# Folding the forward transform over d twice, rounding the spectrum on 128 rows at once, and a product over s1 on alternating halves of the partitions

## The chip, the cores and the metric

One core of one Trainium2 chip runs the whole program. The metric is the device time of one execution in microseconds. Beside it stands the span of one profiled execution, from its first to its last instruction. The engines are named as in the profile: PE is TensorE's matmul, PEld its weight load, DVE is VectorE, ACT is ScalarE, SP is SyncE, which issues most of the DMAs.

## The reference

x has 2048 rows (s) of 576 columns (d). With xn the layer norm of x over d,

```
g = xn @ w_gate ; u = xn @ w_up                  # 576 -> 4608
glu = (sigmoid(g) * u) @ w_down                  # 4608 -> 576
X = rfft2(xn, axes=(s, d)) * (w_r + 1j * w_i)    # 2048 x 289 frequencies
out = x + irfft2(X) + glu
```

All data is float32 and the answer has to be close to float32.

## The kernel before

**Arithmetic.** A float32 matrix is rounded by ACT to a short float that TensorE takes at full rate (the high part), and DVE subtracts it from the original (the low part). A product is three products: high by high, low by high, high by low. Where only 32 rows of the contraction are left (REM), the three are stacked on 96 partitions (KR) and done in one.

**The gated unit** is most of the work: `unit` (L679) runs the products of one block of 128 hidden columns over a half of the rows (L648, 512 columns each), and `down` (L741) and `seven` (L831) the products with w_down (L755 and L846, 288 columns each). They run on PE from the start of the span to its end.

**The spectral branch** runs beside it in the second half of the rows. `begin` (L874) gives the round in which each of its generators starts; in each round every active generator is taken one step further, to its next `yield`. So a `yield` is the distance of one group of 7 matmuls of the gated unit and what goes with it, and the order in which the instructions are written is the order of the rounds. The tile framework then orders each engine's instructions at build time by that order and by its own costs; an instruction whose operands aren't ready there is passed by later ones. On the chip each engine runs its list in order.

`phase1b(t)` (L462) is the forward part for row tile t, of 16: one tile holds two values of s2 with 64 values of s1 each.

- It loads 288 pairs of columns of x, transposed (xs), and the mean of each row spread over the partitions (mb, L467).
- Fold over d (L475 to L477): difference and sum of x[d] and x[575-d], the mean taken off the sums. Of 288 values each 256 lie on 128 partitions twice, 32 on the stacked rows.
- High and low part (fh, fl; L480 to L483).
- Product over d (pd, L486 to L493): for real (e = 0) and imaginary part (e = 1) seven matmuls of 290 columns: two blocks of 128 rows by three, and the 96 stacked rows. The columns are the frequencies, the odd ones first (144), then an empty column that makes 290 of 289, then the 145 even ones. The constants are `cf`.
- Rounding of the spectrum (L496 to L502): pd has s2 and s1 on the partitions and the parts in two PSUM banks. The next product wants part and s1 on the partitions, so four times 64 partitions are moved, each by one ACT (ah) and one DVE instruction (al), scaled by the layer norm's 1/std.
- Product over s1 (pa, L505 to L508): for each of the two s2 three matmuls over 128 partitions, with `am`.
- ACT copies pa to SBUF (L510), and it goes to DRAM (L511).

The tiles pd and pa come from `pair` (L171): two places of two PSUM banks each, shared with the products of L755 and L846.

`phase2` does the sum over s2, the filter and its inverse. `phase3` does the way back; its product over d (pe, L598 to L604) is already folded twice: for each part one matmul of 288 columns over the 102 stacked rows, and six of 144 columns over 128 rows.

At the very start, before x has come, PE multiplies the identity (L902 to L904), some of it with 64 rows: H0 are partitions 0 to 63 and H1 are 64 to 127, taken in turn and written to two different banks.

Of the kernel before, what the change touches and what calls it, by code (L numbers as in the profile page):

```python
# [68 lines left out]
def _constants():  # L69
    out = {}  # L70

    mid = np.arange(HD) - (D - 1) / 2
    ang = 2 * np.pi * mid[:, None] * KOF[None, :] / D
    t = np.zeros((P, 2, 5, NQ), np.float32)
    for e, v in ((0, np.cos(ang)), (1, -np.sin(ang))):
        m = np.where(FREQ, v, 0.0)
        hi, lo = _split(m)
        for part, w in ((0, hi), (1, lo)):
            t[:, e, 2 * part] = w[:P]
            t[:, e, 2 * part + 1] = w[P:2 * P]  # L80
        t[:KR, e, 4] = np.concatenate([hi[2 * P:], hi[2 * P:], lo[2 * P:]])
    out["cf"] = t.reshape(P, 10 * NQ)
# [52 lines left out]
def _layout(x, w_r, w_i, w_gate, w_up, w_down):  # L135
# [11 lines left out]
    lay = {"x": x.reshape(NT, P, D), "xt": xt.reshape(NT, P, 2 * (KT + 1) * P), "xg": xg, "ri": v.reshape(N2 // 2, P, 4 * NQ),  # L147
# [1089 lines left out]
```

## Time and profile before

| | us |
|---|---|
| median of 3 runs (lowest, highest) | 1418.54 (1418.04, 1419.33) |
| the profiled execution | 1417.6 |
| its span | 1415.8 |
| PE busy | 1400.5 (99%) |
| PEld busy | 1228.9 (87%) |
| DVE busy | 1123.7 (79%) |
| ACT busy | 640.3 (45%) |

A matmul's duration in the profile reaches from its issue to the end of its way through the array, and the next one starts before that end. So busy times of PE add up to more than the work, and a cost is read from start to start.

### The profile page before, as it was taken

What the parts mean: (1) busy time and instruction counts of PE and PEld (TensorE: products, weight loads), DVE (VectorE), ACT (ScalarE), POOL (GpSimd) and SP (SyncE); (2) the same over time, 40 slices, a digit from 0 to 9 for tenths busy, and PEclk for the clock granted to TensorE, in tenths of its full rate; (3) what the DMA queues carried; (4) which work ended last, traced back from release to release, by engine and by line L of the source; (5) the groups of instructions that cost most, each with busy time, mean ns of one, the idle gap of its engine ahead of it and who ended that gap; (6) DMA issues with size and microseconds to landing.
All of it is one profiled execution on the core that took longest, in us unless ns stands there. A gap on an engine that the chain in (4) does not pass through costs nothing. (4 is left out here: it accounts for less than half of the span.)

```text
span 1415.8 us, 20731 instructions
## 1 busy us (share of the span) xinstructions
PE 1400.5 (99%) x7883; PEld 1228.9 (87%) x7883; DVE 1123.7 (79%) x1736; ACT 640.3 (45%) x1035; POOL 3.3 (0%) x5
## 2 busy tenths in 40 slices
PE   7999999999999999999999999999999999999998
PEld 5888888888888888888888888888888889888887
DVE  7988888888888888789466888877878878777885
ACT  6644444444444444444245444434555534443431
POOL 0000000000000000000000000000000000000000
PEclk9999999999999999999999999999999999999999
DMA  7588677777777776665777777778888787776643
GB/s 251 194 330 306 257 271 261 271 261 270 262 270 261 272 262 243 246 250 176 274 213 237 225 234 222 219 244 266 274 269 271 241 278 223 242 221 205 194 127 84
DMA packets 131043, 342.54 MB, mean 242 GB/s; under 512 B 12192, under 2 KB 51648, under 8 KB 126208
## 3 DMA queue, kind: packets, MB, share of 16 engines
q1 hardware_dynamic: 130016, 339.91, 71.7%
q8 instruction: 62, 1.02, 0.3%
q10 hardware_dynamic: 928, 1.31, 0.3%
q14 instruction: 37, 0.30, 0.1%
HBM read 205.04 MB, written 136.13 MB: 241 GB/s over the span
## 5 line engine op out<-in xcount | busy, mean ns | idle before, releaser
L648 PE MATMUL pB<-X,w 128*128 128x512 f32 x1484 | 381.0, 394 | 0.9 <-ACT pB L699 0.5
L648 PEld LDWEIGHTS pB<-X,w 128*128 128x128 f32 x1484 | 267.4, 188 | 51.7 <-ACT v L712 1.3
L648 PE MATMUL pE<-X,w 128*128 128x512 f32 x1064 | 272.3, 392 | 0.1
L648 PE MATMUL pA<-X,w 128*128 128x512 f32 x1008 | 259.3, 392 | 1.8 <-DVE X L455 1.2
L648 PEld LDWEIGHTS pE<-X,w 128*128 128x128 f32 x1064 | 193.1, 188 | 35.1 <-DVE y L713 0.7
L648 PEld LDWEIGHTS pA<-X,w 128*128 128x128 f32 x1008 | 182.7, 188 | 35.2 <-DVE X L455 1.9
L755 PE MATMUL po<-wd,hh 128*128 128x288 f32 x1216 | 210.8, 295 | 0.0
L846 PEld LDWEIGHTS ps<-wf,hs 128*128 128x128 f32 x1260 | 188.6, 188 | 18.5 <-ACT qs L854 0.9
L846 PE MATMUL ps<-wf,hs 128*128 128x288 f32 x1260 | 202.0, 295 | 0.4 <-ACT qs L854 0.4
L755 PEld LDWEIGHTS po<-wd,hh 128*128 128x128 f32 x1216 | 184.2, 188 | 11.7 <-ACT hh L738 0.4
L759 DVE TENSOR_TENSOR acc<-acc,po 128x576 f32<-128x576 f32 x168 | 125.7, 749 | 65.4 <-PE po L755 64.9
L250 ACT ACTIVATE w<-raw 128x768 fp32r<-128x768 f32 (+1 forms) x106 | 100.9, 953 | 92.6 <-PE pE L648 36.5
L755 PE MATMUL po<-wd,hl 128*128 128x288 f32 x608 | 128.7, 293 | 0.0
L856 DVE TENSOR_TENSOR qs<-qs,ps 128x576 f32<-128x576 f32 x112 | 84.0, 750 | 25.4 <-PE ps L846 24.4
L755 PEld LDWEIGHTS po<-wd,hl 128*128 128x128 f32 x608 | 98.7, 189 | 0.0
L713 DVE TENSOR_TENSOR y<-v,pE 128x512 f32<-128x512 f32 x68 | 46.6, 686 | 50.3 <-ACT v L712 49.5
L733 DVE TENSOR_TENSOR y<-y,g 128x1024 f32<-128x1024 f32 x67 | 81.9, 1222 | 3.4 <-DVE y L732 0.5
L782 ACT ACTIVATE hs<-y 128x512 fp32r<-128x512 f32 x105 | 64.8, 629 | 43.4 <-DVE y L820 14.8
L252 DVE TENSOR_TENSOR w<-raw,w 128x512 fp32r<-128x512 f32 (+1 forms) x106 | 81.8, 772 | 3.2 <-ACT w L250 2.9
L856 DVE TENSOR_TENSOR acc<-acc,ps 128x576 f32<-128x576 f32 x90 | 67.4, 750 | 19.5 <-PE ps L846 18.6
L716 ACT ACTIVATE g<-pB 128x512 f32<-128x512 f32 x68 | 40.7, 598 | 91.3 <-PE pB L648 91.3
L712 ACT ACTIVATE v<-pB 128x512 f32<-128x512 f32 x68 | 40.6, 597 | 70.5 <-PE pB L648 70.2
(170 smaller groups left out, 1611.0 us busy)
## 6 DMA issues: line engine op xcount, KB each, us to landing
w<-wsp SPq DMA_DIRECT2D x246, 320.0 KB, 3.6
wsp<-w SPq DMA_DIRECT2D x34, 2240.0 KB, 7.8
raw<-in_w SPq DMA_DIRECT2D x34, 768.0 KB, 9.6
wdsp<-wd SPq DMA_DIRECT2D x36, 576.0 KB, 4.6
wf<-tsp SPq DMA_DIRECT2D x60, 288.0 KB, 3.5
wf<-wdsp SPq DMA_DIRECT2D x45, 288.0 KB, 3.9
std<-in_wd SPq DMA_DIRECT2D x36, 288.0 KB, 5.5
ri<-in_ri SPq DMA_DIRECT2D x16, 580.0 KB, 5.1
```

Of the source, the lines that this page charges most:

```text
L250: placed(nc.scalar.activation(o[:, :, :3, :], src, AF.Copy))
L252: placed(nc.vector.tensor_tensor(o[:, :, 3:, :], src[:, :, :KT, :], f32(o[:, :, :KT, :]), op=OP.subtract))
L648: nc.tensor.matmul(bank, w[:, sw, :], X[:, x, sx, :], start=start and j == 0, stop=stop and j == len(STEPS) - 1, skip_group_check=skip)
L712: nc.scalar.activation(v[:, 1], bank["B"], AF.Copy)
L713: nc.vector.tensor_tensor(y[:, 1], v[:, 1], bank["E"], op=OP.add)
L716: nc.scalar.activation(g[:, 1], bank["B"], AF.Sigmoid)
L733: nc.vector.tensor_tensor(y, y, g, op=OP.mult)
L755: nc.tensor.matmul(pd[:, b, :HD], h[i], w[k][b], start=g == 0 and n == 0, stop=g == G - 1 and n == 2)
L759: nc.vector.tensor_tensor(a, a, pd[:, :, :HD], op=OP.add)
L782: nc.scalar.activation(hs[:, 0], src, AF.Copy)
L846: nc.tensor.matmul(pd[:, i, :HD], h[:, a, m], w[:, b], start=q == 0, stop=q == 2)
L856: nc.vector.tensor_tensor(o, o, pd[:, :, :HD], op=OP.add)
```

## The change

The fold is done twice. xs now comes as the four quarters of a row of x (the two that belong together at each level of the fold lie beside each other), and mb is no longer loaded. Two DVE instructions make sums and differences of 512 elements a partition, two of 256 elements and one with the sign column `sg` fold these once more. For each part the odd frequencies need one combination and the even ones the other, so a matmul of 290 columns over 128 rows becomes one of 144 and one of 146 columns, with half the rows in all. The mean only changes frequency 0: DVE takes 576 times the mean from that one column of pd. The spectrum is then rounded by one ACT and one DVE instruction on all 128 partitions. The product over s1 contracts over 64 partitions for one part and one s2 at a time: twelve matmuls instead of six, and from one to the next the half of the partitions and the PSUM bank change.

```diff
     ang = 2 * np.pi * (QTR[:, None] + 0.5) * KOF[None, :] / D     # constants
-    t = np.zeros((P, 2, 5, NQ), np.float32)
+    t = np.zeros((P, 2, 3, NQ), np.float32)
...
+    out["sg"] = np.where(np.arange(P) % REM < REM // 2, 1.0, -1.0).astype(np.float32)[:, None]
...
+    am = am.reshape(2, N1, N2 // 2, 2, 2, P).transpose(3, 1, 2, 0, 4, 5)
...
-    xt = x[:, np.argsort(COLS)].reshape(NT, P, 2, HD)
-    xt = np.stack([xt[:, :, 0], xt[:, :, 1, ::-1]], 2)
-    xt = xt[..., ks].reshape(NT, P, 2, KT + 1, P).transpose(0, 4, 2, 3, 1)
+    qs = np.concatenate([np.arange(P), np.tile(np.arange(P, HQ), P // (HQ - P))])
+    xt = x.reshape(NT, P, 2, 2, HQ)[..., qs].reshape(NT, P, 2, 2, 2, P).transpose(0, 5, 3, 2, 4, 1)
...
     def phase1b(t):
-        pool, cf = R["pool"], R["cf"]
-        xs = pool.tile([P, 2, KT + 1, P], F32, tag="xs", name=f"xs{t}", bufs=2)
-        nc.sync.dma_start(xs.rearrange("p h k s -> p (h k s)"), xt[t])
-        mb = pool.tile([P, P], F32, tag="mb", name=f"mb{t}", bufs=2)
-        nc.sync.dma_start(mb, rowd[0, t].partition_broadcast(P))
+        pool, cf, sg = R["pool"], R["cf"], R["sg"]
+        xs = pool.tile([P, 3, 2, 2 * P], F32, tag="xs", name=f"xs{t}", bufs=2)
+        nc.sync.dma_start(xs[:, :2].rearrange("p h j s -> p (h j s)"), xt[t])
         am = pool.tile([P, 2, 2, P], F32R, tag="am", name=f"am{t}", bufs=2)
         load_r(am, con["am"][:, t * 4 * P:(t + 1) * 4 * P].rearrange("p (a h m) -> p a h m", a=2, h=2))
         yield
         yield
         yield
         yield
-        eo = pool.tile([P, 2, KT + 1, P], F32, tag="eo", name=f"eo{t}")
-        tc.keep_in_program_order(nc.vector.tensor_tensor(eo[:, 1], xs[:, 0], xs[:, 1], op=OP.subtract))
-        nc.vector.scalar_tensor_tensor(xs[:, 0], mb.unsqueeze(1).to_broadcast([P, KT + 1, P]), -2.0, xs[:, 0], op0=OP.mult, op1=OP.add)
-        nc.vector.tensor_tensor(eo[:, 0], xs[:, 0], xs[:, 1], op=OP.add)
-        fh = pool.tile([P, 2, KT + 1, P], F32R, tag="fh", name=f"fh{t}")
-        fl = pool.tile([P, 2, KT, P], F32R, tag="fl", name=f"fl{t}")
+        tc.keep_in_program_order(nc.vector.tensor_tensor(xs[:, 2], xs[:, 0], xs[:, 1], op=OP.add))
+        nc.vector.tensor_tensor(xs[:, 0], xs[:, 0], xs[:, 1], op=OP.subtract)
+        v = xs[:, 0::2]
+        eo = pool.tile([P, 2, 3, P], F32, tag="eo", name=f"eo{t}")
+        six = eo.rearrange("p e c s -> p (e c) s")
+        for o, op in ((six[:, 0::4], OP.add), (six[:, 1::2][:, :2], OP.subtract)):
+            nc.vector.tensor_tensor(o, v[:, :, 0, :P], v[:, :, 1, :P], op=op)
+        nc.vector.scalar_tensor_tensor(eo[:, :, 2], v[:, :, 1, P:], sg, v[:, :, 0, P:], op0=OP.mult, op1=OP.add)
+        fh = pool.tile([P, 2, 3, P], F32R, tag="fh", name=f"fh{t}")
+        fl = pool.tile([P, 2, 2, P], F32R, tag="fl", name=f"fl{t}")
         nc.scalar.activation(fh, eo, AF.Copy)
-        nc.vector.tensor_tensor(fl, eo[:, :, :KT], f32(fh[:, :, :KT]), op=OP.subtract)
+        nc.vector.tensor_tensor(fl, eo[:, :, :2], f32(fh[:, :, :2]), op=OP.subtract)
         r = slice(REM, 2 * REM)
-        nc.vector.tensor_tensor(fh[r, :, KT], eo[r, :, KT], f32(fh[r, :, KT]), op=OP.subtract)
+        nc.vector.tensor_tensor(fh[r, :, 2], eo[r, :, 2], f32(fh[r, :, 2]), op=OP.subtract)
         yield
         yield
         pd = pair(f"pd{t}")
         for e in range(2):
-            steps = []
-            for k in range(2):
-                steps += [(fh[:, e, k, :], cf[:, e, k, :]), (fl[:, e, k, :], cf[:, e, k, :]), (fh[:, e, k, :], cf[:, e, 2 + k, :])]
-            steps.append((fh[:KR, e, KT, :], cf[:KR, e, 4, :]))
-            for n, (l, r) in enumerate(steps):
-                nc.tensor.matmul(pd[:, e, :NQ], l, r, start=n == 0, stop=n == len(steps) - 1)
+            nc.tensor.matmul(pd[:, e, :NQ], fh[:KR, 1 - e, 2, :], cf[:KR, e, 2, :], start=True, stop=False, skip_group_check=True)
+            for c, o in ((0, slice(0, HQ)), (1, slice(HQ, NQ))):
+                for n, (v, i) in enumerate(((fh, 0), (fl, 0), (fh, 1))):
+                    nc.tensor.matmul(pd[:, e, o], v[:, 1 - e, c, :], cf[:, e, i, o], start=False, stop=n == 2, skip_group_check=True)
         ah = pool.tile([P, 2, NQ], F32R, tag="ah", name=f"ah{t}", bufs=1)
         al = pool.tile([P, 2, NQ], F32R, tag="al", name=f"al{t}", bufs=1)
-        for sl in range(2):
+        zero = pd[:, 0, PAD + 1:PAD + 2]
+        nc.vector.scalar_tensor_tensor(zero, mv[:, t, 0:1], float(-D), zero, op0=OP.mult, op1=OP.add)
+        v, r = pd[:, :, :NQ], rstd[:, t:t + 1]
+        nc.scalar.activation(ah, v, AF.Copy, scale=r)
+        nc.vector.scalar_tensor_tensor(al, v, r, f32(ah), op0=OP.mult, op1=OP.subtract)
+        yield
+        yield
+        pa = pair(f"pa{t}")
+        for n, (h, m) in enumerate(((0, ah), (0, al), (1, ah))):
             for ci in range(2):
-                o = slice(ci * N1, (ci + 1) * N1)
-                i = slice(sl * N1, (sl + 1) * N1)
-                v, r = pd[i, ci, :NQ], rstd[i, t:t + 1]
-                nc.scalar.activation(ah[o, sl, :], v, AF.Copy, scale=r)
-                nc.vector.scalar_tensor_tensor(al[o, sl, :], v, r, f32(ah[o, sl, :]), op0=OP.mult, op1=OP.subtract)
-        yield
-        yield
-        pa = pair(f"pa{t}")
-        for sl in range(2):
-            for n, (h, m) in enumerate(((0, ah), (0, al), (1, ah))):
-                nc.tensor.matmul(pa[:, sl, :NQ], am[:, sl, h, :], m[:, sl, :], start=n == 0, stop=n == 2)
+                for sl in range(2):
+                    o = slice(sl * N1, (sl + 1) * N1)
+                    nc.tensor.matmul(pa[:, sl, :NQ], am[o, ci, h, :], m[o, ci, :], start=n + ci == 0, stop=n + ci == 3)
...
     def stage1():
         pool = room("1")
-        R["cf"] = cf = pool.tile([P, 2, 5, NQ], F32R, name="cf")
-        load_r(cf, con["cf"].rearrange("p (e k n) -> p e k n", e=2, k=5))
+        R["cf"] = cf = pool.tile([P, 2, 3, NQ], F32R, name="cf")
+        load_r(cf, con["cf"].rearrange("p (e k n) -> p e k n", e=2, k=3))
+        R["sg"] = sg = pool.tile([P, 1], F32, name="sg")
+        nc.sync.dma_start(sg, con["sg"])
```

## Rows read from the trace of the kernel before

**Rows 1.** The head of the page: span, busy time, share and instructions of each engine
```profile
span 1415.8 us, 20731 instructions
PE 1400.5 (99%) x7883; PEld 1228.9 (87%) x7883; DVE 1123.7 (79%) x1736; ACT 640.3 (45%) x1035; POOL 3.3 (0%) x5
```
**Rows 2.** The page's chain that ended last, by line
```profile
PE ps L846 10%; PE pB L648 10%; PE pE L648 6%; PE pA L648 6%; PE po L755 2%; PE pd L493 2%; PE pe L604 1%; PE pc L548 1%; PE py L575 1%; PE pb L532 1%; PE pa L508 1%; DVE al L502 1%; DVE hs L783 0%; PE pz L588 0%; DVE y L820 0%; PE pe L600 0%
```
**Rows 3.** By stretch: length, busy PE, PEld, DVE, ACT, POOL, clock, DMA share, GB/s
```profile
500.00:700.00 200.00, 199.90 (x1096) 175.63 (x1096) 155.73 (x218) 79.76 (x110) 0.00 (x0) 1.00 0.69 246
...
722.00:937.00 215.00, 213.49 (x1202) 184.47 (x1201) 175.21 (x287) 108.33 (x189) 0.00 (x0) 1.00 0.74 223
```
**Rows 4.** Groups by line, 722 to 937 us: PEld; after the bar busy, mean ns, idle before
```profile
L846 PEld LDWEIGHTS ps<-wf,hs 128*128 128x128 f32 x402 | 59.7, 188 | 6.9 <-ACT qs L854 0.9 <-DVE acc L856 0.8 <-ACT hs L782 0.4
...
L508 PEld LDWEIGHTS pa<-ah,am 128*128 128x128 f32 x64 | 11.3, 188 | 5.7 <-DVE al L502 2.9 <-ACT qs L854 0.9 <-ACT ah L501 0.8
L508 PEld LDWEIGHTS pa<-al,am 128*128 128x128 f32 x32 | 6.0, 189 | 0.8 <-DVE al L502 0.8
```
**Rows 5.** Timeline of PE, product over d of tile 0; columns: start us, length us
```profile
726.96 0.30 PE L493 MATMUL pd<-cf,fh 128*128 128x290 f32 x1
...
728.86 0.39 PE L648 MATMUL pE<-X,w 128*128 128x512 f32 x1
```
**Rows 6.** Busy time of L493, then of L508 alone (PE, PEld), columns as above
```profile
722.00:937.00 215.00, 35.58 (x224) 31.97 (x224) 1.00 0.74 223
...
722.00:937.00 215.00, 17.42 (x96) 13.61 (x96) 1.00 0.74 223
```
**Rows 7.** Timeline of PE, product over s1 of tile 0 and what follows
```profile
735.80 0.29 PE L508 MATMUL pa<-ah,am 128*128 128x290 f32 x1
...
736.62 0.39 PE L648 MATMUL pA<-X,w 128*128 128x512 f32 x1
736.85 0.29 PE L846 MATMUL ps<-wf,hs 128*128 128x288 f32 x1
```
**Rows 8.** Timeline of PE, the way back's product over d of tile 0
```profile
1172.31 0.30 PE L600 MATMUL pe<-drt,z3r 102*128 102x288 f32 x1
...
1172.52 0.27 PE L604 MATMUL pe<-dit,z3l 128*128 128x144 f32 x1
...
1173.08 0.34 PE L600 MATMUL pe<-drt,z3r 102*128 102x288 f32 x1
...
1173.88 0.44 PE L648 MATMUL pB<-X,w 128*128 128x512 f32 x1
```
**Rows 9.** Timelines of PE and PEld at the start, 8 to 10.1 us
```profile
8.02 0.19 PEld L904 LDWEIGHTS b<-idr 64*128 64x128 f32 x2 [0.65 <-issue]
8.36 0.63 PE L904 MATMUL b<-idr 64*128 64x512 f32 x4
8.59 0.83 PE L904 MATMUL b<-idr 64*128 64x512 f32 x3
8.92 0.19 PEld L904 LDWEIGHTS b<-idr 128*128 128x128 f32 x1 [0.37 <-issue]
9.59 0.18 PEld L904 LDWEIGHTS b<-idr 64*128 64x128 f32 x1 [0.37 <-issue]
10.02 0.19 PEld L904 LDWEIGHTS b<-idr 128*128 128x128 f32 x1 [0.24 <-issue]
```
**Rows 10.** Groups by line, 722 to 937 us: DVE and ACT
```profile
L502 DVE SCALAR_TENSOR_TENSOR al<-pd,rstd,ah 64x290 fp32r<-64x290 f32 x64 | 33.2, 519 | 19.5 <-ACT ah L501 18.1
...
L481 DVE TENSOR_TENSOR fl<-eo,fh 128x512 fp32r<-128x512 f32 x16 | 11.0, 687 | 2.0 <-ACT fh L480 1.8
...
L475 DVE TENSOR_TENSOR eo<-xs 128x384 f32<-128x384 f32 x16 | 8.9, 554 | 0.2
...
L501 ACT ACTIVATE ah<-pd,rstd 64x290 fp32r<-64x290 f32 x64 | 31.8, 498 | 46.4 <-PE pd L493 28.9 <-DVE al L502 16.6
...
L510 ACT ACTIVATE x<-pa 128x580 f32<-128x580 f32 x16 | 10.5, 654 | 19.6 <-PE pa L508 13.1 <-issue 6.4
```

More of the change, by code (lines that the diff above doesn't have):

```diff
@@ L70, in _constants @@
     out = {}
-    mid = np.arange(HD) - (D - 1) / 2
-    ang = 2 * np.pi * mid[:, None] * KOF[None, :] / D
-    t = np.zeros((P, 2, 5, NQ), np.float32)
-    for e, v in ((0, np.cos(ang)), (1, -np.sin(ang))):
-        m = np.where(FREQ, v, 0.0)
-        hi, lo = _split(m)
[L78 to L82, printed above, removed]
+    ang = 2 * np.pi * (QTR[:, None] + 0.5) * KOF[None, :] / D
+    t = np.zeros((P, 2, 3, NQ), np.float32)
+    for e, m in ((0, np.cos(ang)), (1, np.sin(ang))):
+        m = np.where(FREQ & (KOF != (HD, 0)[e]), m, 0.0)
+        hi, lo = _split(m)
+        t[:, e, 0], t[:, e, 1] = hi[:P], lo[:P]
+        even, odd = ~ODD, ODD
+        both = []
+        for v in (hi, hi, lo):
+            both += [v[P:] * w.astype(np.float32) for w in ((even, odd) if e == 0 else (odd, even))]
+        t[:KR, e, 2] = np.concatenate(both)
+    out["cf"] = t.reshape(P, 6 * NQ)
+    out["sg"] = np.where(np.arange(P) % REM < REM // 2, 1.0, -1.0).astype(np.float32)[:, None]
     s1 = np.arange(N1)
@@ L142, in _layout @@
     x = x.reshape(S, D)[ROWS][:, COLS]
-    xt = x[:, np.argsort(COLS)].reshape(NT, P, 2, HD)
-    xt = np.stack([xt[:, :, 0], xt[:, :, 1, ::-1]], 2)
-    xt = xt[..., ks].reshape(NT, P, 2, KT + 1, P).transpose(0, 4, 2, 3, 1)
+    qs = np.concatenate([np.arange(P), np.tile(np.arange(P, HQ), P // (HQ - P))])
+    xt = x.reshape(NT, P, 2, 2, HQ)[..., qs].reshape(NT, P, 2, 2, 2, P).transpose(0, 5, 3, 2, 4, 1)
     xg = x.reshape(NT, P, 2, HD)[TPP:, ..., ks].reshape(2, TPC, P, 2, KT + 1, P).transpose(0, 3, 5, 4, 1, 2).reshape(2, 2, P, (KT + 1) * CW)
-    lay = {"x": x.reshape(NT, P, D), "xt": xt.reshape(NT, P, 2 * (KT + 1) * P), "xg": xg, "ri": v.reshape(N2 // 2, P, 4 * NQ),
+    lay = {"x": x.reshape(NT, P, D), "xt": xt.reshape(NT, P, 8 * P), "xg": xg, "ri": v.reshape(N2 // 2, P, 4 * NQ),
            "w": w.reshape(NF, P, 4 * (KT + 1) * P), "wd": w_down[:, COLS].reshape(NF, P, D)}
@@ L487, in phase1b @@
         for e in range(2):
-            steps = []
-            for k in range(2):
-                steps += [(fh[:, e, k, :], cf[:, e, k, :]), (fl[:, e, k, :], cf[:, e, k, :]), (fh[:, e, k, :], cf[:, e, 2 + k, :])]
-            steps.append((fh[:KR, e, KT, :], cf[:KR, e, 4, :]))
-            for n, (l, r) in enumerate(steps):
-                nc.tensor.matmul(pd[:, e, :NQ], l, r, start=n == 0, stop=n == len(steps) - 1)
+            nc.tensor.matmul(pd[:, e, :NQ], fh[:KR, 1 - e, 2, :], cf[:KR, e, 2, :], start=True, stop=False, skip_group_check=True)
+            for c, o in ((0, slice(0, HQ)), (1, slice(HQ, NQ))):
+                for n, (v, i) in enumerate(((fh, 0), (fl, 0), (fh, 1))):
+                    nc.tensor.matmul(pd[:, e, o], v[:, 1 - e, c, :], cf[:, e, i, o], start=False, stop=n == 2, skip_group_check=True)
         ah = pool.tile([P, 2, NQ], F32R, tag="ah", name=f"ah{t}", bufs=1)
         al = pool.tile([P, 2, NQ], F32R, tag="al", name=f"al{t}", bufs=1)
-        for sl in range(2):
-            for ci in range(2):
-                o = slice(ci * N1, (ci + 1) * N1)
-                i = slice(sl * N1, (sl + 1) * N1)
-                v, r = pd[i, ci, :NQ], rstd[i, t:t + 1]
-                nc.scalar.activation(ah[o, sl, :], v, AF.Copy, scale=r)
-                nc.vector.scalar_tensor_tensor(al[o, sl, :], v, r, f32(ah[o, sl, :]), op0=OP.mult, op1=OP.subtract)
+        zero = pd[:, 0, PAD + 1:PAD + 2]
[3 more added lines that the diff above has]
+        nc.vector.scalar_tensor_tensor(al, v, r, f32(ah), op0=OP.mult, op1=OP.subtract)
         yield
@@ L505, in phase1b @@
         pa = pair(f"pa{t}")
-        for sl in range(2):
-            for n, (h, m) in enumerate(((0, ah), (0, al), (1, ah))):
-                nc.tensor.matmul(pa[:, sl, :NQ], am[:, sl, h, :], m[:, sl, :], start=n == 0, stop=n == 2)
+        for n, (h, m) in enumerate(((0, ah), (0, al), (1, ah))):
+            for ci in range(2):
+                for sl in range(2):
+                    o = slice(sl * N1, (sl + 1) * N1)
+                    nc.tensor.matmul(pa[:, sl, :NQ], am[o, ci, h, :], m[o, ci, :], start=n + ci == 0, stop=n + ci == 3)
         x1 = pool.tile([P, 2, NQ], F32, tag="x1", name=f"x1{t}", bufs=1)
```

## The prediction, written before the changed kernel was built or run

> **What bounds the kernel now.** I read the head of the page first: PE is busy for 1400.5 of 1415.8 us, DVE for 79%, ACT for 45% [rows 1]. The chain of waits, followed back from the end, goes through PE's lines, with 1% for the busiest line of another engine [rows 2]. So time is won or lost where PE's instructions get closer or further apart. The table by stretch, of a stretch without the spectral branch and of the one in which phase1b runs, says whether another engine takes over there: PE 213.49 of 215 us, DVE 175 (81%), ACT 108 (50%), DMA share 0.74, the clock at 1.00, which is 2.4 GHz [rows 3]. PE still sets the pace; DVE is near enough to delay it. What PE loses to them is read from the idle time ahead of its weight loads: 6.5 us ahead of the loads of pa, 6.9 us ahead of those of L846 [rows 4]. The forms and start times of the single instructions give the costs below.
>
> **The product over d.** Fourteen matmuls before and after. Before, they start at 726.96 us and the next product at 728.86: 1.90 us, 0.136 each [rows 5]. In ten of the sixteen tiles the first one starts early and the other 13 follow, with another product between, which makes 26 runs. PE's busy time at L493 is 35.58 us; each run reaches 0.16 us over the start of its follower (0.30 of duration less 0.14), so it is (35.58 - 26 x 0.16) / 16 = 1.96 us a tile [rows 5, 6]. After, each part is one matmul of 290 columns over 96 rows, three of 144 and three of 146. This has a twin: the way back's product, one of 288 columns over 102 rows and six of 144, twice, takes 1.57 us [rows 8]. It isn't half: from 1172.52 to 1173.08 five matmuls of 144 columns start, 0.112 us each, against 0.136 for 290 columns, so the narrow ones pay for something other than columns, and 146 should cost as 144 does. The product behind the twin lasts 0.44 instead of 0.39 us: its load comes 0.05 late. So 1.57 + 0.05 = 1.62, and 1.96 - 1.62 = 0.34 a tile, 5.5 us over 16. Ends: 6.2 (1.57) and 2 (the first matmul now needs the last DVE result, the stacked rows' low part, so a load that waits could cost 0.2 a tile more; but until it is ready PE has other products, and the split falls away).
>
> **The product over s1.** Six matmuls become twelve over 64 rows. Before: 0.82 us where nothing waits (735.80 to 736.62) [rows 7]; (17.42 - 19 x 0.16) / 16 = 0.90 on average, in 19 runs [rows 6]. The trace has 64-row matmuls on alternating halves of the partitions and alternating banks at the start, 512 columns wide. Pairs of them start at 8.36 and 8.59 us: 0.23 a pair [rows 9], which is what one over 128 rows takes (736.62 to 736.85) [rows 7]. So the two of a pair run side by side, and twelve of 290 columns cost six passes, 0.82, as before.
>
> Each change of mode costs extra, though. Three pairs take from 8.02 to 8.92, 0.90 us, where 3 x 0.23 = 0.69: 0.21 over. Two matmuls over 128 rows from there to 9.59: 0.67 for 0.46, 0.21 over. One pair from there to 10.02: 0.43 for 0.23, 0.20 over [rows 9]. At every one of these points the load is preceded by an idle time put down to "issue", and isn't ahead of its matmul as elsewhere. One visit is two changes, 0.41 us; 16 visits are +6.6 us.
>
> The Trainium skill has a rule that speaks against this edit: in "TensorEngine Tiling (Array Packing)", under Tiling Modes, Key Properties, it says that changing the tiling mode, other than changing the tile, drains TensorE. The trace agrees, with 0.20 to 0.21 us a change [rows 9]; the page has no price. Without this rule and these rows the switch term would be nothing and the sum below 6.6 us lower, 1410.8.
>
> Two things go with it. First the waits. The 6.5 us of idle loads ahead of pa [rows 4] come from the chain between pd and pa: four ACT copies of 0.498 us and four DVE subtractions of 0.519 in turn [rows 10]. Afterwards it is a tiny DVE instruction, one ACT copy of 580 elements (0.654 as the copy of pa) and one DVE subtraction; DVE's rate between 384 and 512 elements is (687 - 554) / 128 = 1.04 ns an element [rows 10], so it takes 0.519 + 290 x 0.00104 = 0.82 us. 4.1 us of work become 1.6, the distance in the program stays at two yields, and a wait partly falls into the drain. A load normally runs some 0.1 us ahead, so the 6.5 us cost PE less, I estimate 4; I count half of it as gone, -2 us (ends -6.5 and +1). Second, interruptions: the order at build time may put other products between the matmuls of a tile, as before with three extra runs. This was free and now costs two changes. I count two, +0.8 us (ends 0 and one per tile, 6.6).
>
> **DVE, ACT, queues.** DVE a tile: three folds of 0.554 and four subtractions of 0.519, 3.74 us, go [rows 10]; two of 512 elements (0.687), three of 256 (0.554 - 0.133 = 0.42), one of 580 (0.82) and the correction of one column (0.554 - 384 x 0.00104, about 0.16) come: 3.61. The low parts (L481, L483) stay. So DVE is as full as before; its saving is in the handovers, which held it for 18.1 us behind ACT [rows 10]. ACT loses 4 x 0.498 - 0.654 = 1.34 us a tile, 21 us in all, beside an engine that idles half of the stretch [rows 3]: nothing by itself. The fold's chain before fh gets longer by 2 x 0.687 + 3 x 0.42 - 3 x 0.554 = 0.97 us; two yields of PE work hide it, and without that cover it would be 0.97 x 16 = 15 us at most, which PE would fill with later products. A wait is new: ah waits for DVE's correction. Behind ah in ACT's list stand the copies that empty the gated unit's banks, and PE waits for these; the price is what stands ahead of the correction on DVE, one instruction of 0.7 us, against two handovers less. pd and pa take one of the two pair places each; pd's is given back some 2.5 us earlier (4.1 - 1.6), which helps L846, whose loads idle 6.9 us in this stretch [rows 4]. For all this I take -1 us (ends -3 and +1). On SP's queue 16 DMAs of mb go; xs grows from 384 to 512 KB, cf shrinks from 1450 to 870 KB: with a DMA share of 0.74 [rows 3] and four yields of lead, nothing.
>
> **Sum.** -5.5 + 6.6 - 2.0 + 0.8 - 1.0 = -1.1 us. The profiled execution took 1417.6 us, 0.9 below the median of the runs, 1418.54; so 1417.6 becomes 1416.5 and the median 1417.4. This is within 0.2% (2.8 us), about what a measurement of this kernel can tell from no change.
>
> **Rivals.** (A) *The waits go altogether.* The shorter chain takes all 4 us of waiting, no tile is interrupted, L846 gains 2 us: -5.5 + 6.6 - 4 - 2 = -4.9, 1413.6 us. For it: the chain is 2.5 us shorter in every tile. Against it: most idle times ahead of loads are short, and a mode change needs its load late in any case.
>
> (B) *Other products cut the 64-row product in pieces.* It is slower: each cut costs 0.41 us. The forecast has two; from 2 + 1.1 / 0.41, about five, the kernel is slower than before; with one per tile it is 14 x 0.41 = 5.7 more, +4.6, 1423.1 us. For it: the first four matmuls need only ah and the next four al, which comes 0.8 us later, and ten of sixteen tiles of pd were cut at just such a point. Against it: pa was cut in two tiles only.
>
> (C) *The pairs don't run side by side at 290 columns.* Then six passes come on top, 6 x 0.136 x 16 = 13.1 us: 1430.5. The rows at the start speak against it, since the two s2 go to two banks as there.
>
> **How the numbers follow.** Forecast 0.51, A 0.27, B 0.17, C 0.05. The forecast's terms spread by some 2 us: 0.12 of it is faster by over 0.2%, 0.10 slower; of A 0.85 is faster, of B 0.7 slower, C is slower. Faster 0.06 + 0.23 = 0.29, within 0.49, slower 0.05 + 0.12 + 0.05 = 0.22. The range reaches from beyond A, 1411.5, to B, 1423.
>
> **What would show it.** pd starts 14 matmuls in about 1.6 us, the ones of 144 and 146 columns 0.112 apart. pa starts two matmuls at a time, 0.136 apart, with a bare load of "issue" on both sides, about 1.2 us from its first to the next product. ah and al are one instruction each of 0.65 and 0.82 us, and the idle loads of pa and L846 shrink. I am wrong if the change of mode is hidden or dearer than 0.2 us in the midst of work, if pa has many more than 18 runs, or if DVE's idle time turns into waits of PE.

## The result and the profile after

The changed kernel takes 1424.26 us (median of 6 runs, 1423.29 to 1426.01), the kernel before 1418.55 in the same series (1418.04 to 1419.33): a ratio of 1.0041 [1.0028, 1.0054]. It is slower by 5.7 us, and the forecast of 1417.4 and its range missed it.

The head of the page after, for [rows 1]:

```profile
span 1421.8 us, 20844 instructions
PE 1401.3 (99%) x7979; PEld 1227.4 (86%) x7979; DVE 1118.1 (79%) x1736; ACT 621.1 (44%) x987; POOL 3.3 (0%) x5
```

The span is 6.0 us longer and PE's busy time only 0.8: PE didn't get more work, it stood still more. The table by stretch, for [rows 3], says where:

```profile
500.00:700.00 200.00, 199.92 (x1098) 175.62 (x1097) 155.77 (x219) 79.78 (x110) 0.00 (x0) 1.00 0.69 242
722.00:937.00 215.00, 208.33 (x1268) 177.29 (x1267) 168.05 (x285) 88.36 (x139) 0.00 (x0) 1.00 0.74 223
```

Without the branch nothing changed. In phase1b's stretch PE went from 213.49 to 208.33, though DVE went from 175.21 to 168.05 and ACT from 108.33 to 88.36: all three do less in the same time, at the same clock. The groups of weight loads of 722 to 942 us, for [rows 4], whose stretch ends at 937 (last column: idle time ahead of them, and what ended it):

```profile
L850 PEld LDWEIGHTS ps<-wf,hs 128*128 128x128 f32 x397 | 59.3, 188 | 10.8 <-PE pB L652 2.0 <-DVE qs L860 1.9 <-ACT qs L858 0.8
L510 PEld LDWEIGHTS pa<-ah,am 64*128 64x128 f32 x128 | 10.0, 185 | 2.6 <-issue 1.5 <-ACT g L713 0.3 <-ACT pB L703 0.3
L492 PEld LDWEIGHTS pd<-cf,fh 96*128 96x128 f32 x32 | 6.1, 189 | 6.3 <-ACT hs L786 3.0 <-issue 2.6 <-ACT pB L703 0.4
```

pa's idle fell from 6.5 to 2.6, most of it "issue", the change of mode. But L850 (L846 before) went from 6.9 (7.0 up to 942 us) to 10.8, and the stacked rows of pd (L492), without idle time of note before, have 6.3.

**What each product costs PE** can be worked out from start times. For every run of matmuls of pd or pa: from the start of the matmul ahead of it to the start of the second one behind it, less the distance that the two outer ones have when nothing waits (0.227 us for 512 columns, 0.131 for 288: the usual steps of these traces). "Others" is what all other steps of the gated unit between 722 and 942 us have over those distances. In us, for 16 tiles, from the one profiled execution of each kernel; beside it the time (the median of its runs) and its ratio to the kernel before from the same chip:

| kernel | time | ratio | pd | pa | others | sum |
|---|---|---|---|---|---|---|
| before | 1418.55 | 1 | 32.6 | 16.8 | 4.4 | 53.8 |
| after | 1424.26 | 1.0041 [1.0028, 1.0054] | 31.2 | 19.3 | 8.3 | 58.9 |
| e1_old_rounding | 1427.15 | 1.0062 [1.0048, 1.0075] | 28.1 | 19.2 | 14.7 | 62.0 |
| e2_new_rounding_only | 1419.53 | 1.0008 [0.9999, 1.0016] | 31.9 | 19.3 | 3.7 | 54.8 |
| e3_no_correction | 1422.1 | 1.0025 [1.0016, 1.0034] | 31.4 | 19.3 | 6.6 | 57.3 |
| e4_correction_on_act | 1422.7 | 1.0028 [1.0018, 1.0039] | 31.4 | 19.3 | 6.8 | 57.4 |
| e5_stacked_last | 1423.56 | 1.0033 [1.0020, 1.0045] | 29.7 | 19.3 | 8.9 | 57.9 |
| e6_last_and_act | 1422.45 | 1.0023 [1.0013, 1.0032] | 29.7 | 20.0 | 7.4 | 57.0 |
| e7_before_longer_fold | 1419.61 | 1.0010 [1.0002, 1.0019] | 30.9 | 18.7 | 5.9 | 55.6 |
| e9_batch_newround | 1423.59 | 1.0039 [1.0026, 1.0051] | 30.6 | 18.1 | 10.8 | 59.5 |
| e10_fold_a_round_earlier | 1419.88 | 1.0012 [1.0003, 1.0022] | 27.2 | 19.6 | 8.1 | 54.9 |
| e11_earlier_and_act | 1417.66 | 0.9994 [0.9985, 1.0003] | 27.5 | 19.9 | 5.6 | 53.0 |
| e12_no_first_fold | 1415.56 | 0.9985 [0.9976, 0.9994] | 26.1 | 20.0 | 5.4 | 51.5 |
| e13_first_fold_on_pool | 1424.59 | 1.0049 [1.0034, 1.0063] | 25.9 | 19.5 | 7.7 | 53.1 |
| e14_early_act_old_rounding | 1424.15 | 1.0046 [1.0033, 1.0058] | 28.7 | 18.9 | 12.4 | 60.0 |
| e15_before_early | 1419.47 | 1.0004 [0.9995, 1.0013] | 30.5 | 17.4 | 5.8 | 53.7 |

In every kernel but e13 the time less the sum is 1364 to 1366 us: the sum accounts for the differences to about 1 us. From before to after it grows by 5.0 of the 5.7.

**pd** itself came as forecast. PE's timeline of a tile in which nothing waits (start, duration):

```profile
833.40 0.30 PE L492 MATMUL pd<-cf,fh 96*128 96x290 f32 x1
833.54 0.23 PE L495 MATMUL pd<-cf,fh 128*128 128x144 f32 x1
833.61 0.28 PE L495 MATMUL pd<-cf,fl 128*128 128x144 f32 x1
833.72 0.39 PE L495 MATMUL pd<-cf,fh 128*128 128x144 f32 x2
...
834.05 0.28 PE L495 MATMUL pd<-cf,fh 128*128 128x146 f32 x1
834.17 0.34 PE L492 MATMUL pd<-cf,fh 96*128 96x290 f32 x1
...
834.97 0.44 PE L652 MATMUL pB<-X,w 128*128 128x512 f32 x1
```

1.57 us to the next product, whose own duration is 0.44, as at the twin [rows 8]. But only few tiles look so. Another one, all engines:

```profile
846.29 0.41 DVE L487 TENSOR_TENSOR fh<-eo,fh 32x256 fp32r<-32x256 f32 x1
...
846.82 0.19 PEld L492 LDWEIGHTS pd<-cf,fh 96*128 96x128 f32 x1 [0.78 <-issue]
846.86 0.37 PE L492 MATMUL pd<-cf,fh 96*128 96x290 f32 x1 [0.37 <-DVE fh L487]
```

The last instruction of the fold ends at 846.70, and PE, which had nothing else to do, starts 0.16 later. In 10 of the 16 tiles pd starts about 0.15 us behind L487. So of pd's 31.2 us 4.5 lie ahead of its first matmul (0.8 before).

**pa** as forecast too. PE's timeline, and that of its loads:

```profile
839.94 0.54 PE L510 MATMUL pa<-ah,am 64*128 64x290 f32 x4
840.32 0.43 PE L510 MATMUL pa<-al,am 64*128 64x290 f32 x4
840.59 0.43 PE L510 MATMUL pa<-ah,am 64*128 64x290 f32 x4
840.95 0.73 PE L652 MATMUL pA<-X,w 128*128 128x512 f32 x2
```

```profile
839.94 0.30 PEld L510 LDWEIGHTS pa<-ah,am 64*128 64x128 f32 x4 [0.16 <-issue]
...
840.95 0.53 PEld L652 LDWEIGHTS pA<-X,w 128*128 128x128 f32 x3 [0.17 <-issue]
```

From its first matmul to the next product it is 1.01 us (the forecast's sign was about 1.2), four matmuls in 0.27 (840.32 to 840.59), so the pairs do run side by side; a bare load stands on both sides. By the accounting, which also counts the idle time ahead of the first matmul, each of the 16 tiles costs 1.20 to 1.21 us, against 0.80 to 0.83 before where a tile wasn't cut and nothing waited. None is cut in pieces.

**The correction comes late.** Tile 7, DVE, ACT and PE; pd's last matmul ends at 822.23:

```profile
822.91 0.69 DVE L824 TENSOR_TENSOR y<-y 128x512 f32<-128x512 f32 x1
823.57 0.69 DVE L787 TENSOR_TENSOR hs<-y,hs 128x512 fp32r<-128x512 f32 x1
824.18 0.16 DVE L499 SCALAR_TENSOR_TENSOR pd<-mv,pd 128x1 f32<-128x1 f32 x1
...
824.37 0.74 ACT L501 ACTIVATE ah<-pd,rstd 128x580 fp32r<-128x580 f32 x1 [0.83 <-DVE pd L499]
...
825.57 0.81 DVE L502 SCALAR_TENSOR_TENSOR al<-pd,rstd,ah 128x580 fp32r<-128x580 f32 x1
...
826.49 0.90 PE L850 MATMUL ps<-wf,hs 128*128 128x288 f32 x5 [0.91 <-PE pB L652]
```

The correction of one column, 0.16 us, stands behind two instructions of 0.69 for the gated unit and starts 1.95 us after pd. al ends at 826.38 and gives back the pair place; L850 starts 0.11 later. The wait is put down to PE, but PE had nothing under way: it is the place. In tiles 0, 1, 4, 7, 10 and 14 the place is held (from pd's first matmul to the end of al) for 5.6 to 6.5 us, in the others for 3.6 to 4.7, and the six long waits of L850 (0.28 to 1.65 us, 4.35 in all) stand at those six.

But only three of the six, in tiles 1, 4 and 7 with 1.83 us together, end behind al, 0.10 to 0.15 us after it. The other three, with 2.52 us, end 0.05 us behind the copy or the sum that empties the *other* pair place, while al isn't done. The longest is at tile 10, where this sum (L860) stands late in DVE's list and ends at 868.82:

```profile
868.07 0.75 DVE L860 TENSOR_TENSOR qs<-qs,ps 128x576 f32<-128x576 f32 x1
...
868.87 1.05 PE L850 MATMUL ps<-wf,hs 128*128 128x288 f32 x6 [1.49 <-DVE qs L860]
```

The one at tile 0 (0.50 us) was there in the kernel before, too (0.61). ACT's list of waits from 722 to 940 us (in total, times, longest):

```profile
ACT ah L501 <- DVE pd L499: 23.9, 13, 3.9
```

### The profile page after: what moved, and what is told of

Its sections match the earlier page's. It is cut to its first block, busy times and chain, and to the rows that moved or that the text cites. A ratio compares the mean times of both kernels' runs of the same rounds, so it can differ in the third digit from the quotient of the medians.

```text
span 1421.8 us, 20844 instructions
## 1 busy us (share of the span) xinstructions
PE 1401.3 (99%) x7979; PEld 1227.4 (86%) x7979; DVE 1118.1 (79%) x1736; ACT 621.1 (44%) x987; POOL 3.3 (0%) x5
## 4 chain that ended last, share of the span: by engine, by line
PE 89%; DVE 8%; ACT 1%; issue 1%; DMA 0%; ACTq 0%; DVEq 0%
PE pB L652 23%; PE po L759 18%; PE pE L652 15%; PE pA L652 15%; PE ps L850 11%; PE pe L606 1%; PE pd L495 1%; PE pc L550 1%; PE py L577 1%; PE pb L534 1%; DVE hs L787 1%; PE pa L510 1%; DVE y L824 1%; DVE y L737 1%; DVE acc L860 0%
## 5 line engine op out<-in xcount | busy, mean ns | idle before, releaser
L850 PEld LDWEIGHTS ps<-wf,hs 128*128 128x128 f32 x1260 | 188.9, 188 | 22.5 <-PE pB L652 2.0
L850 PE MATMUL ps<-wf,hs 128*128 128x288 f32 x1260 | 202.0, 295 | 3.4 <-DVE qs L860 1.5
L860 DVE TENSOR_TENSOR qs<-qs,ps 128x576 f32<-128x576 f32 x112 | 84.0, 750 | 31.5 <-PE ps L850 30.9
L717 DVE TENSOR_TENSOR y<-v,pE 128x512 f32<-128x512 f32 x68 | 46.6, 686 | 54.6 <-ACT v L716 53.8
L860 DVE TENSOR_TENSOR acc<-acc,ps 128x576 f32<-128x576 f32 x90 | 67.4, 749 | 22.0 <-PE ps L850 21.6
L787 DVE TENSOR_TENSOR hs<-y,hs 128x512 fp32r<-128x512 f32 x105 | 71.2, 686 | 4.5 <-ACT hs L786 3.8
```

What stands on the lines that cost most here:

```text
L717: nc.vector.tensor_tensor(y[:, 1], v[:, 1], bank["E"], op=OP.add)
L787: return lambda: nc.vector.tensor_tensor(hs[:, 1], src, f32(hs[:, 0]), op=OP.subtract)
L850: nc.tensor.matmul(pd[:, i, :HD], h[:, a, m], w[:, b], start=q == 0, stop=q == 2)
L860: nc.vector.tensor_tensor(o, o, pd[:, :, :HD], op=OP.add)
```

## The experiments

**Which half of the change costs?** One part at a time: in e1 the new fold with the old rounding, in e2 the old fold with the new rounding.

```diff
 e1, of after:
-        v, r = pd[:, :, :NQ], rstd[:, t:t + 1]
-        nc.scalar.activation(ah, v, AF.Copy, scale=r)
-        nc.vector.scalar_tensor_tensor(al, v, r, f32(ah), ...)
+        (the loops over sl and ci with 64 partitions each, and the product over s1
+         with six matmuls on 128 rows, as before)
 e2, of before: the same edit the other way round
```

> The change with the rounding and the product over s1 of before (four pieces of 64 partitions, six matmuls over 128 rows); the second fold and the correction on DVE stay. Theory, three separate costs in PE's time of this stretch: the product over s1 +2.5 us (6.4 of mode changes less 3.9 of waits that went), the late first matmul of the product over d +3.7, the waits of L850 behind DVE's correction +4.1. By it this run takes 1424.3 - 2.5 = 1421.8 us, its product over s1 back at about 1.05 us a tile, and L850's waits as long as in the change. Rival, that the 64-row product is the whole loss and the rest follows from it: 1418 us or less, with L850's waits as short as before.

> The kernel before with the rounding on 128 rows and the 64-row product over s1 alone; the fold, the mean's broadcast and the product over d as before, no correction. Theory of three costs: only the product over s1 is dearer, 1418.5 + 2.5 = 1421.0 us, about 1.21 us a tile, and L846's waits no longer than before, since nothing of DVE stands between the product over d and its rounding. Rival, that the mode changes throw PE's list out of step with the others: 1424 to 1425, with L846's waits some 4 us longer.

e2 is the new rounding with its changes of mode by itself: pa +2.5 us by the accounting, about +1.1 in time (1.0008 [0.9999, 1.0016]), no difference that the runs can tell. e1, which I expected to be better than after, is rather worse: 1.0062, with intervals that just overlap, and 3.1 us more in the sum. The stacked rows wait less there (pd 28.1), but the gated unit lost 14.7, and pa costs 19.2 without any change of mode (1.20 us a tile; I had expected 1.05). The loads of e1 in 722 to 942 us:

```profile
L851 PEld LDWEIGHTS ps<-wf,hs 128*128 128x128 f32 x378 | 53.4, 188 | 15.2 <-DVE acc L861 6.5 <-DVE qs L861 2.7 <-ACT x L513 2.2
```

9.2 of these 15.2 us are put down to the gated unit's own sums on DVE (L861). The place of pd is held for 8.2 us there, hardly shorter than in the kernel before (8.4), which waits for much less: the hold by itself doesn't explain it. So the loss comes with the fold, and with the fold the new rounding does better than the old one; that the changes of mode made the kernel slow fell.

**Is it the correction's place on DVE?** e3 leaves the correction out (the mean then stays in frequency 0). e4 does it on ACT, right ahead of ah, with a constant made once:

```diff
 e3: the line is deleted; e4:
-        nc.vector.scalar_tensor_tensor(zero, mv[:, t, 0:1], float(-D), zero, op0=OP.mult, op1=OP.add)
+        nc.scalar.activation(zero, zero, AF.Identity, bias=R["nd"][:, t:t + 1])
 in stage1:
+        R["nd"] = nd = pool.tile([P, NT], F32, name="nd")
+        nc.vector.tensor_scalar(nd, mv[:, :, 0], float(-D), None, op0=OP.mult)
```

> The change without the correction of frequency 0, so the mean's share of that frequency is left out of the computation; all else stays. Theory, that the correction's place in DVE's list keeps the pair place and lets L850 wait: 4 us fewer, 1420.3, the product over d is rounded within 0.2 us of its end in every tile, and L850 waits as before. Rival, that L850 waits because DVE is late anyway (longer fold): no change, 1424.

> The change with the correction done by ACT just ahead of its copy (a bias of -576 times the mean, made once for all tiles) instead of by DVE. Theory as for the run without correction: DVE no longer stands between the product and the copy, so 1420.5 us, with one more short ACT instruction a tile. Rival, that any second step between product and rounding costs the same, or that ACT's copies for the gated unit stand behind it: 1424.

1.0025 and 1.0028 against 1.0041: 2.2 and 1.8 us of it (0.0016 and 0.0013 of 1418), with intervals that just overlap. The accounting has the same size, 1.6 and 1.5, and in the right place: L850's part of "others" (its steps that are over 0.05 us late) goes from 4.9 to 2.9 and 3.3 us. The longest wait, at tile 10, stays in e4 (1.67 us), as its releaser says. So the late correction is about a third of the loss.

**Is it that the stacked rows come first?** e5 puts their matmul behind the six others; e6 is e5 with e4.

```diff
-            nc.tensor.matmul(pd[:, e, :NQ], fh[:KR, 1 - e, 2, :], cf[:KR, e, 2, :], start=True, stop=False, ...)
 (the six, the first of them now with start=True)
+            nc.tensor.matmul(pd[:, e, :NQ], fh[:KR, 1 - e, 2, :], cf[:KR, e, 2, :], start=False, stop=True, ...)
```

> The change with the matmul over the stacked rows as the last of each part's seven (as before) instead of the first. In the change the product over d starts 0.15 us after the stacked rows' low part, DVE's last instruction of the fold, in eleven of sixteen tiles, and PE loses 4.5 us ahead of it, where the kernel before lost 0.8, since its first matmul needs only the high parts. Theory, that the order of these seven is the cause: 3 us fewer than the change, 1421.3, with the first matmul starting ahead of the stacked rows again in about ten tiles. Rival, that the fold's chain is simply later (five DVE instructions ahead of ACT's instead of three), and PE waits for it wherever the stacked rows stand: within 1 us of 1424.3, the wait before the second matmul instead of the first.

> The change with the stacked rows last and the correction done by ACT: both suspected waits at once. If they are two separate costs, 3 + 1.6 us fewer than the change: 1419.7 us. If they are one (DVE late), about 1422, as with ACT's correction alone. Below 1418 only if the product over d keeps all of its 5 us and L850's waits go as well.

Little: 1.0033 and 1.0023, within the intervals of after and e4; in e5 the sum has 1.6 us less at pd and 0.6 more at the others. The wait moved by one matmul. The loads of e5:

```profile
L494 PEld LDWEIGHTS pd<-cf,fl 128*128 128x128 f32 x64 | 12.2, 191 | 2.0 <-DVE fl L485 1.7
```

The low part that the second matmul needs is itself late. So the order in pd is at most a small part; the whole fold ends too late.

**Does a longer chain cost by itself?** e7 is the kernel before, with its last fold instruction (L477) executed three times: 2 x 0.554 us longer, the same result.

```diff
         nc.vector.tensor_tensor(eo[:, 0], xs[:, 0], xs[:, 1], op=OP.add)
+        nc.vector.tensor_tensor(eo[:, 0], xs[:, 0], xs[:, 1], op=OP.add)
+        nc.vector.tensor_tensor(eo[:, 0], xs[:, 0], xs[:, 1], op=OP.add)
```

> The kernel before with the last of its three fold instructions done three times (the same result; 2 x 0.55 us more on DVE a tile, all ahead of ACT's high part), nothing else. It lengthens the chain by as much as the second fold does (0.97 us by my sum), with the old product and rounding behind it. Theory that the chain's length alone does little, because the first matmuls need only the high parts and other products fill in: 1418.5 to 1420. Rival, that a longer chain on DVE costs PE 4 us wherever the first matmul stands: 1422.

1.0010 [1.0002, 1.0019]: 1.4 us for 17.7 us of DVE's time. PE's list then splits pd in 14 tiles instead of 10 (30 runs), and a product of the gated unit fills the gap between the first matmul, which needs only fh, and the others. But e7 lengthened more than the chain: from the fold's first instruction to pd's first matmul it is 6.8 us there (median of the tiles) and 4.1 in the kernel before, so the order made at build time gave the longer chain more lead as well. By the accounting pd costs 1.7 us less, and pa (48 runs instead of 19) and the others 3.4 more. With that lead and that split a longer chain costs little; what it costs without them, e7 doesn't show.

**Could fewer changes of mode pay?** e9 is e2 with two tiles a visit: 8 visits instead of 16.

```diff
+        held.append((t, am, ah, al))
+        if t % 2 == 0:
+            return
+        (24 matmuls for both tiles into two pair places, then both copies; ah, al twice)
```

> The kernel before with the rounding on 128 rows and the 64-row product over s1, and that product done for two tiles at a time, 24 matmuls in one visit: 8 visits instead of 16 (ah and al get a second place each, am a third). Theory that each visit costs two changes of mode, 0.41 us: 8 x 0.41 = 3.3 us fewer than the run with 16 visits (1419.5), 1416.2, below the kernel before. Rival, that both pair places taken at once let L846 wait for as much: 1419 or more, with longer waits there.

pa falls from 19.3 to 18.1, but a visit takes both pair places until ACT has emptied them:

```profile
L853 PEld LDWEIGHTS ps<-wf,hs 128*128 128x128 f32 x396 | 58.9, 188 | 14.0 <-ACT x L517 7.9 <-issue 1.3 <-DVE al L501 0.4
```

1.0039 against e2's 1.0008: 4.4 us worse. The rival won.

**The fold earlier.** If it ends too late, starting it one round earlier must help: e10 moves one `yield` from ahead of the fold to behind it, and changes nothing else. e11 is e10 with e4. e15 is the control: the same move in the kernel before.

```diff
         yield
         yield
         yield
-        yield
         tc.keep_in_program_order(nc.vector.tensor_tensor(xs[:, 2], ...))
 ...
         nc.vector.tensor_tensor(fh[r, :, 2], eo[r, :, 2], f32(fh[r, :, 2]), op=OP.subtract)
         yield
         yield
+        yield
         pd = pair(f"pd{t}")
```

> The change with the fold written one round (one yield) earlier: three rounds behind its loads instead of four, and three ahead of the product over d instead of two. Nothing is computed otherwise. Theory, that PE's waits ahead of and inside the product over d (4.5 us ahead of it in the change, 1.4 ahead and 2 inside with the stacked rows last) come from the fold's longer chain being late: they go, 1424.3 - 4 = 1420.3 us, the first matmul more than 0.5 us behind the stacked rows in nearly every tile. Rival, that DVE's list as a whole is late and the fold only one of the places where it shows: the waits move to L850, 1423 or more.

> The change with the fold one round earlier and the correction done by ACT. Two separate costs: 1424.3 - 4 - 1.6 = 1418.7 us, level with the kernel before; the product over d then costs PE some 27 us in all 16 tiles against 32.6 before, the product over s1 19.3 against 16.8. Below 1417 only if L850's waits are no longer than before. If DVE's list as a whole is late: 1421 to 1422, as with either of the two alone.

> The kernel before with its fold one round earlier, nothing else: the control for the earlier fold. There PE loses 0.8 us ahead of the product over d, and about 0.1 us for each of ten interrupted tiles. If the earlier fold only takes away waits for the fold: 1 to 2 us fewer at most, 1416 to 1418. If it gains as much here (4 us, 1414), its gain in the changed kernel says nothing of the second fold.

e10: 1.0012 against 1.0041, 4.1 us back, and the accounting puts 4.0 of it at pd (31.2 to 27.2). Same tile as above, in e10:

```profile
841.32 0.41 DVE L486 TENSOR_TENSOR fh<-eo,fh 32x256 fp32r<-32x256 f32 x1
...
842.64 0.19 PEld L492 LDWEIGHTS pd<-cf,fh 96*128 96x128 f32 x1
...
842.77 0.30 PE L492 MATMUL pd<-cf,fh 96*128 96x290 f32 x1
...
844.35 0.44 PE L652 MATMUL pB<-X,w 128*128 128x512 f32 x1
```

The fold is ready 1.04 us ahead, and pd takes 1.58. In the kernel before, the move gains nothing (1.0004 [0.9995, 1.0013]): no tile of pd is split any more, which takes 2.1 us off pd, but pa and the others cost 2.0 more. So the gain in time isn't one that any kernel would have had. e11 takes away both delays: 0.9994 [0.9985, 1.0003], 1417.66 us, the level of the kernel before.

**What would DVE's time be worth?** e12 is e4 without the first level of the fold (its two instructions of 512 elements are left out, and the second level reads the input as it is). e13 is e11 with these two on GpSimd. e14 is e11 with the old rounding, like e1.

```diff
 e13:
-        tc.keep_in_program_order(nc.vector.tensor_tensor(xs[:, 2], xs[:, 0], xs[:, 1], op=OP.add))
-        nc.vector.tensor_tensor(xs[:, 0], xs[:, 0], xs[:, 1], op=OP.subtract)
+        tc.keep_in_program_order(nc.gpsimd.tensor_tensor(xs[:, 2], xs[:, 0], xs[:, 1], op=OP.add))
+        nc.gpsimd.tensor_tensor(xs[:, 0], xs[:, 0], xs[:, 1], op=OP.subtract)
```

> The change with the correction done by ACT and without the first level of the fold: its two DVE instructions of 512 elements are left out, the second level works on the raw halves, so the spectrum is another one. 1.37 us a tile less on DVE and in the chain. Theory that the fold's chain is what makes PE wait for the product over d: those 4.6 us go, 1422.7 - 4.5 = 1418.2. Rival, that the 64-row product's place in PE's list is at fault: 1422.

> The change with the fold one round earlier, the correction done by ACT, and the two instructions of the fold's first level done by GpSimd, which is idle in this stretch, instead of DVE. No row here has such an instruction on GpSimd, so its length is open. If DVE's load is what matters and GpSimd is done within the round (2.2 us): some 2 us fewer than the same kernel with the fold on DVE, 1416 to 1417. If it takes longer than a round, the product over d waits again: 1421 or more.

> The second fold with all waits that were found taken away and without changes of mode: the fold one round earlier, the correction on ACT, the rounding in four pieces and the product over s1 over 128 rows as before. If the fold is worth its 5 us where nothing waits, and the 64-row product costs PE the 2.5 us that were read from it: product over d 27 us, over s1 17 to 18, waits of L846 about 5, against 32.6, 16.8 and 4.4 before: 1417.8 - 4 = 1414 us, faster than both kernels and some 3 us below the same kernel with the 64-row product (1417.7). Rival, that the four pieces keep the pair place for 7 to 10 us as in the first run of this study and L846 waits for it by 10 us: 1420 or more.

e12: 0.9985 [0.9976, 0.9994], 6.1 us below e4's ratio: 1.37 us of DVE's time a tile, 22 us in all, is worth 6, though DVE was busy for only 168.05 of 215 us of that stretch in the changed kernel. It can't tell DVE's load from the chain's length, since it shortens both; 5.3 of the 6.0 us by which the sum falls are pd's. It is the only one below before, and it leaves work out.

e13 missed: 1.0049. Not in phase1b's stretch, where its sum is 53.1 like e11's, but ahead of it, as its table by stretch shows (PE, PEld, DVE, ACT, POOL, clock):

```profile
705.00:710.00 5.00, 1.83 (x14) 1.56 (x12) 3.65 (x4) 0.33 (x1) 3.85 (x3) 0.94 0.03 11
710.00:715.00 5.00, 4.65 (x16) 4.36 (x17) 3.97 (x8) 0.99 (x2) 1.50 (x2) 0.50 0.68 229
715.00:720.00 5.00, 5.00 (x31) 4.58 (x31) 3.09 (x4) 0.30 (x1) 4.50 (x3) 0.88 0.52 170
```

```profile
706.36 2.88 DVE L479 TENSOR_TENSOR eo<-xs 128x256 f32<-128x256 f32 x2 [3.53 <-POOL xs L474]
709.16 0.47 DVE L480 SCALAR_TENSOR_TENSOR eo<-xs,sg 128x256 f32<-128x256 f32 x1
709.55 0.74 DVE L765 TENSOR_TENSOR acc<-acc,po 128x576 f32<-128x576 f32 x1
```

The second fence is DVE's timeline. DVE's list has the first tile's second level ahead of the gated unit's sum (L765). DVE waits 3.53 us there for GpSimd, and its two L479 then take 2.88 us beside GpSimd's next two instructions (0.84 in e11). The products behind L765 wait for all that: PE stands for 3.5 us. After that the granted clock is 0.50 (1.2 GHz) from 710 to 715 us and 0.88 from 715 to 720; an estimate from these shares is 2.5 + 0.6 us lost. Together 6.6 of the 6.9 us between e13 and e11.

e14, which I expected below e11, is 6.5 us above it: "others" 12.4, nearly as in e1. Its rival came true in the time and in the hold of pd's place (8.2 us), but that hold is again no longer than in the kernel before. Twice the old rounding went badly with the new fold, and both times I had expected the opposite.

## Why the prediction was wrong

Sum of the forecast: -1.1 us. Measured: +5.7. By its steps:

- **pd's matmuls: right.** Without the time ahead of the first one, pd took 31.8 us before and 26.7 after: -5.1, forecast -5.5. 1.67 a tile, forecast 1.62; always one run.
- **"The fold's chain before fh gets longer by 0.97 us; two yields of PE work hide it": the step that failed.** The length wasn't the error: from the fold's first instruction to fh it takes 4.02 us in the median tile, 3.67 before, and to the stacked rows 5.47, 5.03 before. (The means, 6.40 and 5.18 to the stacked rows, are carried by tiles 1 to 3, whose folds are spread over 9.8 to 14.2 us; before, only tile 3's is, over 9.8.) But the cover wasn't there. pd used to start with fh and needed the stacked rows last; now its first matmul needs them, 1.4 us behind fh, and no other product stands in between: 4.5 us are lost ahead of pd, and pd gained 1.4 instead of 5.5. e10 shows it: with one round more of cover 4.0 us come back at that place. What I overlooked was in the trace of before (ACT, DVE, PE and its loads in one of the ten split tiles):

```profile
842.46 0.85 ACT L480 ACTIVATE fh<-eo 128x768 fp32r<-128x768 f32 x1 [0.91 <-DVE eo L477]
...
843.36 0.19 PEld L493 LDWEIGHTS pd<-cf,fh 128*128 128x128 f32 x1 [0.32 <-ACT fh L480]
843.36 0.40 PE L493 MATMUL pd<-cf,fh 128*128 128x290 f32 x1
...
843.60 1.09 PE L648 MATMUL pB<-X,w 128*128 128x512 f32 x4
843.61 0.68 DVE L481 TENSOR_TENSOR fl<-eo,fh 128x512 fp32r<-128x512 f32 x1
844.32 0.41 DVE L483 TENSOR_TENSOR fh<-eo,fh 32x256 fp32r<-32x256 f32 x1
...
844.53 0.29 PE L493 MATMUL pd<-cf,fl 128*128 128x290 f32 x1
```

  pd starts 0.05 us after fh is done (843.31), goes on 0.24 after fl (844.29), and reaches the stacked rows last. In all ten split tiles the first matmul follows fh by 0.05 to 0.26 us: the fold was on the edge already, and the split was the cover, with another product in the gap. I read it as a cost that would fall away. With it came the last of the signs of being wrong that the prediction names, waits of PE for DVE. The loads that wait were an end of pd's range (0.2 a tile), and 0.23 a tile came.
- **Mode changes: right.** 1.21 - 0.81 = 0.40 us a tile, 6.4 in all, forecast 6.6. The Trainium skill's rule in "TensorEngine Tiling (Array Packing)", Tiling Modes, Key Properties, holds: a change of tiling mode drains TensorE, and here that is a bare load of 0.16 and 0.17 us idle on the two sides. Rival C is out.
- **pa's waits: mis-sized.** All 3.9 us of them went (16.8 less 16 x 0.81), I had counted half; and no tile was cut, I had counted two. pa came out at +2.5 us, forecast +5.4. This part of rival A is what happened; rival B's cuts are out.
- **DVE, ACT and the pair places: wrong sign.** Forecast -1.0, "others" rose by 3.9. The durations were right but for two: al 0.821 (forecast 0.82), correction 0.16 (0.16), the folds 0.684 to 0.688 and 0.420; ah took 0.742 (0.65) and the fold with `sg` 0.478 (0.42). A pair place of pd is held for 4.7 us on average instead of 8.4, more than forecast. But I priced the wait for the correction at "one instruction of 0.7 us, against two handovers less"; in 8 tiles it was 0.7 to 2.0 us, and three of L850's long waits end with the hold that this lengthens. e3 and e4 show some 2 us of this. The rest is mostly the gated unit's own sums, late on DVE (tiles 10 and 14, 2.0 us); why the list has them late is open.

The terms together: -1.4 + 2.5 + 3.9 = 5.0, and 0.7 elsewhere. With both delays taken away (e11) the terms are -5.1, +3.1 and +1.2, -0.8 in all, and the time is 1417.66, near the forecast of 1417.4, in part because errors of pa and of "others" cancel.

**Open:** how much the gated unit waits depends on how the rounding is cut (e1 and e14 against after and e11, 6 to 7 us in "others") in a way that I couldn't predict. The order of DVE's list is fixed at build time, and every edit reorders it for other reasons than the chip's; that the order is the cause is argued, not shown.

## What to carry to other kernels

Where an engine's work for a branch is written into the list of an engine that is busy for 80%, the distance to its consumer is what the list gives it, not the sum of its durations; read from the trace how late the last operand comes before the edit, and take a product that is split around a late operand as a sign that the cover is already used up. Put a tiny instruction on the engine that needs its result, and give a lengthened chain one more round of lead with the same edit. A helper engine that is to relieve a busy one must not stand ahead of the critical work in that one's list.

## What the runs showed of the hardware

Matmuls of 144 and 146 columns on 128 rows start 0.11 us apart, hardly less than 290 columns on 96 or 128 rows in the kernel before (0.13 to 0.14). The Trainium skill's "TensorE: Matmul & The Clock Gate" has a figure in its section on LDWEIGHTS that lies near it, the load's columns by 1.2 in ns: 107 ns for 128, an estimate from that page. The loads of pd do follow one another at 0.112 us, but each is recorded with 0.19 us; that the load sets the distance is not shown.

Beside GpSimd, DVE's instructions with two inputs in SBUF take longer. DVE's groups of e11 and then of e13, 722 to 942 us:

```profile
L502 DVE SCALAR_TENSOR_TENSOR al<-pd,rstd,ah 128x580 fp32r<-128x580 f32 x16 | 13.1, 820 | 12.8 <-ACT ah L501 12.7
...
L484 DVE TENSOR_TENSOR fl<-eo,fh 128x512 fp32r<-128x512 f32 x16 | 11.0, 687 | 6.4 <-ACT fh L483 6.4
```

```profile
L502 DVE SCALAR_TENSOR_TENSOR al<-pd,rstd,ah 128x580 fp32r<-128x580 f32 x16 | 13.1, 820 | 1.6 <-ACT ah L501 1.3
L484 DVE TENSOR_TENSOR fl<-eo,fh 128x512 fp32r<-128x512 f32 x15 | 12.7, 850 | 15.7 <-ACT fh L483 15.7
```

fl goes from 687 to 850 ns in the mean, while al, with one input in PSUM, has 820 in both. The mean hides two cases: in e13 the 12 fl with no GpSimd instruction beside them take 688 ns, the four that overlap one 1.01 to 1.82 us. The longest of them, with GpSimd's timeline and DVE's:

```profile
880.08 1.29 POOL L474 TENSOR_TENSOR xs<-xs 128x512 f32<-128x512 f32 x1
880.09 1.82 DVE L484 TENSOR_TENSOR fl<-eo,fh 128x512 fp32r<-128x512 f32 x1 [1.24 <-ACT fh L483]
```

The Trainium skill's "GPSIMD Engine Reference", Specifications, says the same: GpSimd's way to SBUF is shared with VectorE, and instructions with two SBUF inputs contend.
